# RetNet attention and a GELU feed-forward on one core: block 1's first product by seven products in all four pairs, with its sums begun earlier

## The chip, the core and the metric

The kernel runs on one core of one Trainium2 chip. The metric is the device time of one execution in microseconds (us). All data is float32.

The core has five engines with an instruction queue each. TensorE (PE in the profile) multiplies matrices, VectorE is DVE, ScalarE is ACT, GpSimd is POOL, and SyncE (SP) here only issues transfers (DMAs). POOL and ACT issue some transfers too. Each engine executes its queue in order, and an instruction that waits holds up those behind it.

## What is computed

Four batches, eight heads, 768 steps, 64 dimensions per head. First a recurrent attention, then a feed-forward with a quick GELU:

```
state = gamma[h] * state + outer(k[t], v[t])       # per batch and head, 64 x 64
y[t]  = scale * q[t] @ state
x     = y, heads side by side: 3072 tokens x 512
h     = x @ w_in                                    # 512 x 2048
g     = h * sigmoid(1.702 * h)
out   = g @ w_out                                   # 2048 x 512
```

The two weights are given in float64 and are narrowed to float32 on the chip.

## The kernel before

**Attention in steps.** The attention is computed in 24 steps; a step covers 64 time steps of two batches and all heads. `attend` (L281) holds the matmuls of a step: of step j the scores, and of step f the outputs and the state's increment. `turn` (L241) brings q and k into the transposed layout, from step 6 on with two DVE transposes (L253). `decay` (L263) scales k for the state and `aged` (L351) scales the state; both run on POOL from step 6 on (L274 and L359). `masked` (L316), `updated` (L362), `by_state` (L321) and `output` (L333) run on DVE; `output(f)` writes the step's share of x. Four steps fill a block of 512 columns of x, so there are six blocks.

**Products of a block.** A block goes through a first product (with w_in) and a second (with w_out). Weights and x are seen as 2 x 2 blocks, and instead of eight products of blocks seven are enough if sums of blocks are multiplied. From block 2 on `up(d)` (L539) does so for each of four pairs d of feature groups, and `down49` (L627) even in two levels. Block 0's first product is done plainly by `up0` (L407), its second by `down(0)` (L746).

**Block 1's first product.** It has two forms before. `up1(f)` (L420) is plain: four matmuls with 512 columns for one feature group, for f = 8 to 11, which is pair 2. Pairs 0, 1 and 3 go by `seven(d, k)` (L464): part k of pair d is four matmuls with 256 columns, recorded as eight. The parts 0, 2, 4 and 6 accumulate in one PSUM buffer "x", and after part 0, 2 and 4 ACT copies it away (L479, "kept": p1, u and vv) before the next part adds to it. Parts 1, 3 and 5 have buffers of their own, which DVE adds to the copies (L488, L494, L498, L499). `hidden` (L390) is the activation, called a gate.

`up1` and `seven` read x of block 1 from `X1`, which is W2[:, 6]. Its first half comes from steps 4 and 5, its second from steps 6 and 7. The part of the sums of x is made by `seven_x` (L433): four DVE subtractions (L439). The sums of the weights are made without DVE: `seven_w(d)` (L441) lets ACT copy three weight blocks with a sign (L450) and POOL issues DMAs that add another block to the copy (L452): w4, w6, and w5, which adds w4 and therefore waits for it to land. `seven_v(d)` (L454) copies w5 (L459) and adds a fourth block by DMA (L460): w2. Parts 2 to 5 read w5, w4, w6 and w2 in this order.

**Narrowing.** A group of weights passes through `fetch` (SP, L180, two transfers of 512 KB), `abs` (ACT, L207), `half` (three DVE operations, L211 to L213) and `rest` (three, L217 to L222). The raw weights land in three buffers in turn, so that a fetch waits for the `rest` three groups before. w0 to w7 are w_in's pairs and w8 to w15 are w_out's rows.

**The order.** Up to the end of block 1's first product the order is written out by hand: a string of names (L928 to L945), each of which calls one function. `pin` (L118) holds an instruction in this order on its engine. Operations that are not pinned are placed by a scheduler; before the change the POOL operations of `decay` and `aged` are of this kind. Behind the string, `down(0)` begins with PE at L783, and DVE makes the sums of w_out (L521 to L526) and of block 0's g (L530 to L532).

Of the kernel before, what the change touches and what calls it, by code (L numbers as in the profile page):

```python
# [12 lines left out]
ALU = mybir.AluOpType  # L13
P = 128
# [14 lines left out]
def kernel(  # L29
# [29 lines left out]
    pe, act, dve, pool, sp = nc.tensor, nc.scalar, nc.vector, nc.gpsimd, nc.sync  # L59
    ctx.enter_context(tc.manual_schedule(engines={mybir.EngineType.PE}))  # L60

    B, H, S, D = q.shape
    NT, DM = out.shape
    DFF = moe_w_in.shape[1]
    HP = H // 2
# [38 lines left out]
    cold = const.tile([P, 2 * H], F32, name="cold")  # L104
    whole = const.tile([P, HP], F32, name="whole")
    whole_h = const.tile([P, H], F32, name="whole_h")
# [5 lines left out]
    def w1(p):  # L112

        return (W1A, p) if p < NP // 2 else (W1B[p // 2 - 2], p % 2)
# [3 lines left out]
    def pin(i):  # L118
        return tc.keep_in_program_order(i) if ordered[0] else i
# [107 lines left out]
    QT, KT, KD, AT, TURNED, PA, PU, PY, SHARE = [{} for _ in range(9)]  # L227
# [3 lines left out]
    def home(j, name):  # L231

        at = ["qT", "kT", "kd", "at"].index(name)
        shape = [[HP, P] if j < NEW else [H, D]] * 2 + [[H, D], [2, HP, D]]
        shape = shape[at]
        if j >= 2 * CB:
            return one.tile([P] + shape, F32, name=name, tag=name, bufs=[2, 1, 1, 2][at])
        t = G[:, at, j % 2 * 2:j % 2 * 2 + 2].rearrange("p s t -> p (s t)")
        return t.rearrange("p (a b c) -> p a b c", a=2, b=HP) if at == 3 else t.rearrange("p (a b) -> p a b", a=shape[0])
# [23 lines left out]
    def decay(j):  # L263

        if j % NC == NC - 1:
            return
        KD[j] = home(j, "kd")
        x = QKV["kn", j]
        if j < NEW:

            for h in range(H):
                pin(act.activation(KD[j][:, h], x[:, h % HP * 2 + h // HP], AF.Copy, scale=cold[:, H + h:H + h + 1]))
        else:
            pool.tensor_mul(KD[j].rearrange("p (i s) d -> p i s d", i=2), x.rearrange("p (i s) d -> p i s d", i=2),  # L274
                            cold[:, None, H:H + HP, None].to_broadcast([P, 2, HP, D]))

    def by_half(t, j):

# [72 lines left out]
    def aged(f):  # L351

        c = f % NC
        old, new = state[c % 2], state[(c + 1) % 2]
        if f < NEW:
            for s in range(HP):
                pin(act.activation(new[:, :, s], old[:, :, s], AF.Copy, scale=whole[:, s:s + 1]))
        else:
            pool.tensor_mul(new.rearrange("p r s d -> p (r s) d"), old.rearrange("p r s d -> p (r s) d"),  # L359
                            whole_h[:, :, None].to_broadcast([P, H, D]))  # L360

    def updated(f):  # L362
        c = f % NC
# [67 lines left out]
    SUM_X, SUM_W = {}, {}  # L431
# [9 lines left out]
    def seven_w(d):  # L441

        t, q1 = w1(2 * d)
        w = [t[:, q1:q1 + 2, s].rearrange("p u c f -> p u (c f)") for s in range(4)]
        SUM_W[d] = {4: one.tile([P, 2, 2 * P], F32, name="w4", tag="qT", bufs=2),
                    5: one.tile([P, 2, 2 * P], F32, name="w5", tag="at", bufs=2),
                    6: two.tile([P, 2, 2 * P], F32, name="w6", tag="o")}
        m = SUM_W[d]
        for to, of, sign in ((4, 2, 1.0), (6, 2, -1.0), (5, 0, -1.0)):
            pin(act.activation(m[to], w[of], AF.Copy, scale=sign))  # L450
        for to, of in ((m[4], w[3]), (m[6], w[0]), (m[5], m[4])):
            pin(pool.dma_start(to, of, accum_op=ALU.add))  # L452

    def seven_v(d):  # L454

        t, q1 = w1(2 * d)
        m = SUM_W[d]
        m[2] = one.tile([P, 2, 2 * P], F32, name="w2", tag="kT")
        pin(act.activation(m[2], m[5], AF.Copy, scale=-1.0))  # L459
        pin(pool.dma_start(m[2], t[:, q1:q1 + 2, 1].rearrange("p u c f -> p u (c f)"), accum_op=ALU.add))  # L460
# [3 lines left out]
    def seven(d, k):  # L464

        t, q1 = w1(2 * d)
        a = [G[:, 2 * d:2 * d + 2, s, :] for s in range(4)]

        def product(acc, sa, sb, start, stop):
            for u in range(2):  # L470
                for c in range(2):
                    w = SUM_W[d][sa][:, u, c * P:(c + 1) * P] if sa in (4, 5, 6, 2) else t[:, q1 + u, sa, c, :]
                    x = SUM_X[sb][:, c, :] if sb in SUM_X else X1[:, sb, c, :]
                    pe.matmul(acc[:, u, :], w, x, start=(start and u == 0 and c == 0), stop=(stop and c == 1),  # L474
                              skip_group_check=True)

        def kept(name, tag, src):
            SEVEN[name] = one.tile([P, 2, TH], F32, name=name, tag=tag)
            pin(act.activation(SEVEN[name], src, AF.Copy))  # L479

        if k in (0, 1, 3, 5):
            SEVEN["x" if k == 0 else f"y{k}"] = ps.tile([P, 2, TH], F32, name="ph", tag="x" if k == 0 else "y")
        acc = SEVEN[f"y{k}" if k in (1, 3, 5) else "x"]
        product(acc, (0, 1, 5, 4, 6, 2, 3)[k], (0, 1, 5, 4, 6, 3, 2)[k], k in (0, 1, 3, 5), k in (1, 3, 5, 6))
        if k == 0:
            kept("p1", "s1", acc)
        elif k == 1:
            pin(dve.tensor_add(a[0], acc, SEVEN["p1"]))  # L488
        elif k == 2:
            kept("u", "s2", acc)  # L490
            hidden(a[0], a[0])
        elif k == 3:
            SEVEN["t"] = one.tile([P, 2, TH], F32, name="t", tag="s1")
            pin(dve.tensor_add(SEVEN["t"], acc, SEVEN["u"]))  # L494
        elif k == 4:
            kept("vv", "s3", acc)
        elif k == 5:
            pin(dve.tensor_add(a[3], SEVEN["y3"], SEVEN["vv"]))  # L498
            pin(dve.tensor_add(a[2], acc, SEVEN["t"]))  # L499
        else:  # L500
            for s in (3, 2):
                hidden(a[s], a[s])
            hidden(a[1], acc)
# [321 lines left out]
    works, products = {}, {}  # L825
# [72 lines left out]
        works[f"step-{j}"] = lambda j=j: attend(None, j)  # L898
    works["seven_x"] = seven_x
    for d in range(NP // 2):  # L900
        works |= {f"seven_w{d}": lambda d=d: seven_w(d), f"seven_v{d}": lambda d=d: seven_v(d)}
        for n in range(7):
            works[f"seven{d}.{n}"] = lambda d=d, n=n: seven(d, n)
    for i in range(2 * NFF):
        works[f"w{i // 2}{'ab'[i % 2]}"] = lambda i=i: fetch(i)
    for name, i in [("0a", 0), ("0b", 1)] + [(str(p), 2 * p) for p in range(1, NFF)]:
        n = Narrow(i)
# [20 lines left out]
    for name in """  # L928
        k0 table q0 warm turn0 w0b rows warm k1 abs0b q1 turned0 step0 v0 w0a half0b mask k2 turn1 causal rest0b
        masked0 decay0 v1 decay1 abs0a half0a step-0 updated0 turned1 q2 step1 rowd whole w2b turn2 w2a x0 k3  # L930
        aged1 masked1 turned2 v2 rest0a abs2 q3 step-1 updated1 state1 decay2 aged2 step2 q4 x1 half2 decay3 w3b
        w3a up0.0.0 masked2 turn3 k4 step-2 v3 q5 rest2 k5 gate0.0.0 turned3 updated2 state2 step3 up0.0.2
        masked3 abs3 half3 x2 rest3 turn4 w1b step-3 aged3 gate0.0.2 turned4 state3 w1a w5b updated3 v5 decay4
        abs1 x3 turn5 half1 up0.0.3 turned5 up0.1.2 step4 aged4 w5a rest1 v4 gate0.0.3 decay5 w6a masked4
        gate0.1.2 abs5 w6b step5-4 half5 rest5 up0.0.1 updated4 abs6 state4 gate0.0.1 w4b
        up0.1.1 half6 aged5 w4a up0.0.5 rest6 masked5 up0.1.5 gate0.1.1 x4 gate0.0.5 abs4 step-5 w8b w8a
        half4 gate0.1.5 state5 updated5 anew q6 up0.1.6 x5 rest4 gate0.1.6 abs8 v6 up0.0.6 w7b w7a half8
        turn6 gate0.0.6 up0.1.0 abs7 half7 gate0.1.0 w9b w9a up0.1.4 q7 gate0.1.4 decay6 step6 masked6 rest7 up0.0.4 v7
        gate0.0.4 turn7 up0.1.3 gate0.1.3 aged6 step7-6 masked7 updated6 decay7 abs9 state6 x6 up0.0.7 rest8 gate0.0.7
        w11a w11b step-7 state7 x7 seven_w0 half9 w10b w10a up0.1.7 rest9 gate0.1.7 seven_x abs11 half11  # L940
        up1.8 gate1.8 seven_v0 w12a w12b rest11 up1.9 gate1.9 abs10 seven_w1 half10 up1.10 gate1.10 w14b w14a rest10
        up1.11 abs12 gate1.11 seven0.0 seven0.1 half12 w13a w13b seven0.2 seven0.3 rest12 abs14 seven0.4 seven0.5
        half14 seven0.6 aged7 seven_v1 w15a w15b qk8 seven1.0 seven1.1 abs13 rest14 seven1.2 seven1.3 updated7 half13
        seven_w3 seven1.4 seven1.5 abs15 rest13 seven1.6 seven_v3 seven3.0 seven3.1 half15 seven3.2 seven3.3 rest15
        seven3.4 seven3.5 seven3.6 late_loads  # L945
    """.split():
        works[name]()
    ordered[0] = False
# [92 lines left out]
```

## Time and profile before

| | us |
|---|---|
| median of 3 runs | 664.78 (663.43 to 670.63) |
| the profiled execution | 664.22 |
| its span | 662.5 |
| PE busy in the span | 642.5 |
| DVE busy | 444.8 |
| POOL busy | 202.6 |
| ACT busy | 159.1 |
| PE at block 1's first product | 101.13 to 157.01 |

Positions are microseconds from the start of the span. A row of a timeline gives the start, the time to the end of the last instruction in the row, the engine, the line, what is written and read, the shape and the number of records; in brackets stands the idle time ahead of it and what ended it. A row of a stretch gives its length, then for each engine the busy time and the number of instructions, then the TensorE clock that was granted, the share of the 16 DMA engines that was busy, and GB/s.

### The profile page before, as it was taken

What the parts mean: (1) busy time and instruction counts of PE and PEld (TensorE: products, weight loads), DVE (VectorE), ACT (ScalarE), POOL (GpSimd) and SP (SyncE); (2) the same over time, 40 slices, a digit from 0 to 9 for tenths busy, and PEclk for the clock granted to TensorE, in tenths of its full rate; (3) what the DMA queues carried; (4) which work ended last, traced back from release to release, by engine and by line L of the source; (5) the groups of instructions that cost most, each with busy time, mean ns of one, the idle gap of its engine ahead of it and who ended that gap; (6) DMA issues with size and microseconds to landing.
All of it is one profiled execution on the core that took longest, in us unless ns stands there. A gap on an engine that the chain in (4) does not pass through costs nothing.

```text
span 662.5 us, 15229 instructions
## 1 busy us (share of the span) xinstructions
PE 642.5 (97%) x6366; PEld 573.6 (87%) x6366; DVE 444.8 (67%) x634; ACT 159.1 (24%) x306; POOL 202.6 (31%) x228
## 2 busy tenths in 40 slices
PE   7799999899999999999999999999999999999997
PEld 3678885788888888888999888999888999988997
DVE  3799878899735774456985445995254995254965
ACT  4774232552000000333100234010233110233110
POOL 7300321240278217100536500345600255500000
PEclk9899999899999999999999999999999999999999
DMA  9995639774403546272385832295652243602142
GB/s 184 224 258 156 190 77 265 183 147 69 76 23 141 155 120 183 52 252 96 93 221 132 268 72 96 81 219 131 200 153 96 68 148 107 228 26 96 50 158 96
DMA packets 148965, 92.65 MB, mean 140 GB/s; under 512 B 131648, under 2 KB 135232, under 8 KB 147872
## 3 DMA queue, kind: packets, MB, share of 16 engines
q1 hardware_dynamic: 135856, 45.19, 29.9%
q0 software_dynamic: 10704, 45.24, 21.2%
q10 hardware_dynamic: 2336, 1.25, 0.6%
q8 instruction: 50, 0.82, 0.5%
q14 instruction: 19, 0.16, 0.1%
HBM read 72.89 MB, written 15.47 MB: 133 GB/s over the span
## 4 chain that ended last, share of the span: by engine, by line
PE 77%; DMA 8%; issue 5%; DVE 4%; SPq 2%; POOL 2%; ACT 1%; POOLq 0%; ACTq 0%; DVEq 0%
PE pq L650 24%; PE px L546 16%; PE pd L783 13%; PE py L546 12%; PE ph L414 3%; PE ph L474 2%; PE pa L289 2%; DMA w<-w 2%; DMA G<-in_moe_w_in_dram 2%; PE py L312 1%; DMA W<-in_moe_w_out_dram 1%; PE py L306 1%; PE pa L297 1%; SPq L140 1%; DMA k_sq<-in_k_dram 1%
## 5 line engine op out<-in xcount | busy, mean ns | idle before, releaser
L619 POOL DMA_DIRECT2D ring<-W2D x28 | 15.4, 551 | 227.8 <-PE px L546 118.0
L650 PE MATMUL pq<-W,G 128*128 128x128 f32 x672 | 80.2, 276 | 0.0
L650 PEld LDWEIGHTS pq<-W,G 128*128 128x128 f32 x672 | 77.6, 192 | 0.6
L546 PE MATMUL px<-X,W1A 128*128 128x256 f32 x256 | 59.9, 379 | 0.8 <-POOL X L516 0.8
L546 PE MATMUL px<-X,W1B 128*128 128x256 f32 x256 | 59.8, 379 | 0.0
L650 PE MATMUL pq<-ring,own 128*128 128x128 f32 x448 | 59.8, 276 | 0.0
L546 PEld LDWEIGHTS px<-X,W1A 128*128 128x128 f32 x256 | 48.3, 190 | 7.6 <-POOL X L516 1.2
L650 PEld LDWEIGHTS pq<-ring,own 128*128 128x128 f32 x448 | 54.5, 192 | 0.4
L546 PEld LDWEIGHTS px<-X,W1B 128*128 128x128 f32 x256 | 48.6, 190 | 6.7
L393 ACT ACTIVATE G<-G 128x512 f32<-128x512 f32 x57 | 35.7, 630 | 59.2 <-DVE G L556 33.4
L783 PE MATMUL pd<-W,G 128*128 128x256 f32 x224 | 49.6, 381 | 0.0
L783 PEld LDWEIGHTS pd<-W,G 128*128 128x128 f32 x224 | 42.2, 190 | 5.9
L546 PE MATMUL py<-X,W1A 128*128 128x256 f32 x192 | 45.4, 379 | 0.0
L546 PE MATMUL py<-X,W1B 128*128 128x256 f32 x192 | 45.4, 379 | 0.0
L546 PEld LDWEIGHTS py<-X,W1A 128*128 128x128 f32 x192 | 36.5, 190 | 5.0
L546 PEld LDWEIGHTS py<-X,W1B 128*128 128x128 f32 x192 | 36.5, 190 | 5.0
L564 DVE TENSOR_TENSOR t<-py,u 128x512 f32<-128x512 f32 x16 | 11.1, 692 | 33.4 <-PE py L546 33.4
L553 ACT ACTIVATE p<-px 128x512 f32<-128x512 f32 x16 | 9.6, 597 | 94.5 <-PE px L546 94.5
L414 PE MATMUL ph<-X,W1A 128*128 128x256 f32 x128 | 29.0, 382 | 1.1 <-DVE X L347 0.8
L578 DVE TENSOR_TENSOR G<-G 128x512 f32<-128x512 f32 (+2 forms) x24 | 12.3, 514 | 25.7 <-ACT G L393 25.7
L650 PE MATMUL pq<-ring,G 128*128 128x128 f32 x224 | 29.6, 275 | 0.0
L650 PE MATMUL pq<-W,own 128*128 128x128 f32 x224 | 29.6, 275 | 0.0
(234 smaller groups left out, 1214.0 us busy)
## 6 DMA issues: line engine op xcount, KB each, us to landing
ring<-W2D POOLq DMA_DIRECT2D x28, 768.0 KB, 5.0
W1B<-W1D POOLq DMA_DIRECT2D x6, 1792.0 KB, 9.5
W<-in_moe_w_in_dram SPq DMA_DIRECT2D x12, 512.0 KB, 6.6
W<-in_moe_w_out_dram SPq DMA_DIRECT2D x10, 512.0 KB, 5.5
out_dram<-o POOLq DMA_DIRECT2D x20, 256.0 KB, 3.6
q_sq<-in_q_dram SPq DMA_DIRECT2D x144, 32.0 KB, 2.4
k_sq<-in_k_dram SPq DMA_DIRECT2D x144, 32.0 KB, 2.2
v_in<-in_v_dram SPq DMA_DIRECT2D x72, 64.0 KB, 3.2
```

The lines of the kernel that those rows point to most:

```text
L140: keep(engine.dma_start(*((to, at) if name == "v" else (to[:, n:H:2], at[:, n * HP:(n + 1) * HP]))))
L289: pe.matmul(pa[HALF[w], u, 0, s, :], kt[HALF[u], w, s, :], qt[HALF[u], w, s, :], start=True, stop=True)
L393: pin(act.activation(g, h[:, i], AF.Gelu_apprx_sigmoid))
L414: pe.matmul(h[:, ab], w, X[:, 2 * th + c // 2, c % 2, :], start=(ab == 0 and c == 0), stop=(c == 3), skip_group_check=True)
L474: pe.matmul(acc[:, u, :], w, x, start=(start and u == 0 and c == 0), stop=(stop and c == 1), skip_group_check=True)
L546: pe.matmul(acc[:, u, :], t[:, q1 + u, sa, c, :], X[:, sb, c, :], start=(start and u == 0 and c == 0), stop=(stop and c == 1), skip_group_ ...
L553: act.activation(p1, x, AF.Copy)
L564: dve.tensor_add(tt, z, u)
L578: dve.tensor_sub(q[0][1], q[0][0], q[0][1])
L619: pool.dma_start(c, W2D[i])
L650: pe.matmul(p0[:, j, :], a[:, d], w[:, d], start=(new and j == 0 and d == 0), stop=(d == NP // 2 - 1), skip_group_check=True)
L783: pe.matmul(p0[:, n, :], g1(m, p, sa)[:, n * P:(n + 1) * P], W2[:, sb, p, :], start=(new and p == 0 and n == 0), stop=(last and p == NP - ...
```

## The change

Pair 2 of block 1's first product goes by `seven` too, and as the first of the four, so that the order of pairs is 2, 0, 1, 3; `up1` is no longer called. `seven_w` is split: it keeps the three ACT copies, `seven_s` issues the adding DMAs of w4 and w6, and `seven_u` that of w5. For pairs 2 and 0 these stand among block 0's first product, between steps 5 and 7. `seven_x` stands right behind `output(7)` ("x7"), ahead of half9. `decay` and `aged` are pinned on POOL from step 6 on. In the string the narrowing of w9 to w15 is spread anew among the parts of `seven`.

```diff
--- before.py
+++ after.py
@@ -271,8 +271,8 @@
             for h in range(H):
                 pin(act.activation(KD[j][:, h], x[:, h % HP * 2 + h // HP], AF.Copy, scale=cold[:, H + h:H + h + 1]))
         else:
-            pool.tensor_mul(KD[j].rearrange("p (i s) d -> p i s d", i=2), x.rearrange("p (i s) d -> p i s d", i=2),
-                            cold[:, None, H:H + HP, None].to_broadcast([P, 2, HP, D]))
+            pin(pool.tensor_mul(KD[j].rearrange("p (i s) d -> p i s d", i=2), x.rearrange("p (i s) d -> p i s d", i=2),
+                                cold[:, None, H:H + HP, None].to_broadcast([P, 2, HP, D])))
 
     def by_half(t, j):
 
@@ -356,8 +356,8 @@
             for s in range(HP):
                 pin(act.activation(new[:, :, s], old[:, :, s], AF.Copy, scale=whole[:, s:s + 1]))
         else:
-            pool.tensor_mul(new.rearrange("p r s d -> p (r s) d"), old.rearrange("p r s d -> p (r s) d"),
-                            whole_h[:, :, None].to_broadcast([P, H, D]))
+            pin(pool.tensor_mul(new.rearrange("p r s d -> p (r s) d"), old.rearrange("p r s d -> p (r s) d"),
+                                whole_h[:, :, None].to_broadcast([P, H, D])))
 
     def updated(f):
         c = f % NC
@@ -448,8 +448,16 @@
         m = SUM_W[d]
         for to, of, sign in ((4, 2, 1.0), (6, 2, -1.0), (5, 0, -1.0)):
             pin(act.activation(m[to], w[of], AF.Copy, scale=sign))
-        for to, of in ((m[4], w[3]), (m[6], w[0]), (m[5], m[4])):
-            pin(pool.dma_start(to, of, accum_op=ALU.add))
+
+    def seven_s(d):
+
+        t, q1 = w1(2 * d)
+        for to, of in ((4, 3), (6, 0)):
+            pin(pool.dma_start(SUM_W[d][to], t[:, q1:q1 + 2, of].rearrange("p u c f -> p u (c f)"), accum_op=ALU.add))
+
+    def seven_u(d):
+
+        pin(pool.dma_start(SUM_W[d][5], SUM_W[d][4], accum_op=ALU.add))
 
     def seven_v(d):
 
@@ -898,7 +906,8 @@
         works[f"step-{j}"] = lambda j=j: attend(None, j)
     works["seven_x"] = seven_x
     for d in range(NP // 2):
-        works |= {f"seven_w{d}": lambda d=d: seven_w(d), f"seven_v{d}": lambda d=d: seven_v(d)}
+        works |= {f"seven_{n}{d}": lambda d=d, do=do: do(d)
+                  for n, do in (("w", seven_w), ("s", seven_s), ("u", seven_u), ("v", seven_v))}
         for n in range(7):
             works[f"seven{d}.{n}"] = lambda d=d, n=n: seven(d, n)
     for i in range(2 * NFF):
@@ -934,15 +943,15 @@
         abs1 x3 turn5 half1 up0.0.3 turned5 up0.1.2 step4 aged4 w5a rest1 v4 gate0.0.3 decay5 w6a masked4
         gate0.1.2 abs5 w6b step5-4 half5 rest5 up0.0.1 updated4 abs6 state4 gate0.0.1 w4b
         up0.1.1 half6 aged5 w4a up0.0.5 rest6 masked5 up0.1.5 gate0.1.1 x4 gate0.0.5 abs4 step-5 w8b w8a
-        half4 gate0.1.5 state5 updated5 anew q6 up0.1.6 x5 rest4 gate0.1.6 abs8 v6 up0.0.6 w7b w7a half8
-        turn6 gate0.0.6 up0.1.0 abs7 half7 gate0.1.0 w9b w9a up0.1.4 q7 gate0.1.4 decay6 step6 masked6 rest7 up0.0.4 v7
-        gate0.0.4 turn7 up0.1.3 gate0.1.3 aged6 step7-6 masked7 updated6 decay7 abs9 state6 x6 up0.0.7 rest8 gate0.0.7
-        w11a w11b step-7 state7 x7 seven_w0 half9 w10b w10a up0.1.7 rest9 gate0.1.7 seven_x abs11 half11
-        up1.8 gate1.8 seven_v0 w12a w12b rest11 up1.9 gate1.9 abs10 seven_w1 half10 up1.10 gate1.10 w14b w14a rest10
-        up1.11 abs12 gate1.11 seven0.0 seven0.1 half12 w13a w13b seven0.2 seven0.3 rest12 abs14 seven0.4 seven0.5
-        half14 seven0.6 aged7 seven_v1 w15a w15b qk8 seven1.0 seven1.1 abs13 rest14 seven1.2 seven1.3 updated7 half13
-        seven_w3 seven1.4 seven1.5 abs15 rest13 seven1.6 seven_v3 seven3.0 seven3.1 half15 seven3.2 seven3.3 rest15
-        seven3.4 seven3.5 seven3.6 late_loads
+        half4 gate0.1.5 state5 updated5 anew q6 up0.1.6 x5 rest4 gate0.1.6 seven_w2 abs8 v6 decay6 aged6 seven_s2 up0.0.6 w7b w7a half8
+        turn6 gate0.0.6 up0.1.0 abs7 half7 gate0.1.0 seven_w0 seven_u2 seven_s0 w9b w9a up0.1.4 q7 gate0.1.4 step6 masked6 rest7 up0.0.4 v7
+        gate0.0.4 turn7 up0.1.3 gate0.1.3 step7-6 masked7 updated6 decay7 aged7 seven_u0 abs9 state6 x6 up0.0.7 rest8 gate0.0.7
+        w11a w11b step-7 seven_v2 state7 x7 seven_x half9 w10b w10a up0.1.7 gate0.1.7
+        seven2.0 seven2.1 abs11 rest9 seven2.2 w12a w12b seven2.3 half11 seven2.4 abs10 seven2.5 rest11 seven2.6 seven_v0
+        w14b w14a seven0.0 seven0.1 half10 seven0.2 seven_w1 seven_s1 seven0.3 rest10 abs12 seven0.4 seven_u1 seven0.5 half12
+        w13a w13b seven0.6 seven_v1 qk8 rest12 w15a w15b seven1.0 seven_w3 seven_s3 seven1.1 abs14 seven1.2 seven1.3 half14
+        seven1.4 abs13 seven_u3 seven1.5 updated7 rest14 half13 seven1.6 seven_v3 seven3.0 seven3.1 seven3.2 abs15 seven3.3
+        rest13 seven3.4 seven3.5 half15 seven3.6 rest15 late_loads
     """.split():
         works[name]()
     ordered[0] = False
```

## The prediction

> **What bounds the kernel now.** I read the page first, then the timeline of TensorE, the waits, the timelines of POOL, SP and DVE, and stretches of the clock and the DMA share.
>
> ```profile
> span 662.5 us, 15229 instructions
> PE 642.5 (97%) x6366; PEld 573.6 (87%) x6366; DVE 444.8 (67%) x634; ACT 159.1 (24%) x306; POOL 202.6 (31%) x228
> ```
>
> TensorE (PE) is busy for 97% of the span: only fewer PE columns or fewer PE stalls can shorten it. The PE timeline of block 1's first product, with idle time ahead of a row in brackets:
>
> ```profile
> 101.13 13.90 PE L427 MATMUL ph<-W,W1B 128*128 128x512 f32 x32
> 114.87 3.62 PE L474 MATMUL ph<-W,W1A 128*128 128x256 f32 x16
> 121.11 7.13 PE L474 MATMUL ph<-x,w 128*128 128x256 f32 x24 [2.63 <-ACT p L479]
> 131.53 3.62 PE L474 MATMUL ph<-W,W1A 128*128 128x256 f32 x16
> 134.99 5.34 PE L474 MATMUL ph<-x,w 128*128 128x256 f32 x24
> 148.28 5.45 PE L474 MATMUL ph<-x,w 128*128 128x256 f32 x24 [1.04 <-ACT p L479]
> 157.01 3.62 PE L783 MATMUL pd<-W,W1A 128*128 128x256 f32 x16
> ```
>
> Pair 2 takes 114.87 - 101.13 = 13.74 us plainly. Pair 1, undisturbed, takes seven parts of 1.73 us (143.62 - 131.53 = 12.09). Pair 0 stalls for 2.6 us, and its next 24 records take 7.13 us instead of 5.34: the clock fell.
>
> ```profile
> 122.00:124.00 2.00, 2.00 (x6) 1.56 (x6) 2.00 (x3) 0.00 (x0) 0.89 (x1) 0.50 0.60 92
> ```
>
> The third number from the end is the granted clock, 0.50. The blame on the copy p (L479) is only the last link: ACT executes in order, and w2's copy (L459) stood ahead of p, waiting for an adding DMA that POOL had issued late:
>
> ```profile
> 97.55 2.54 POOL L452 DMA_DIRECT2D w<-W1A  x2 [3.50 <-ACT w L450]
> 107.56 0.88 POOL L452 DMA_DIRECT2D w<-w  x1 [7.47 <-issue]
> 143.68 0.90 POOL L452 DMA_DIRECT2D w<-w  x1 [1.26 <-DMA w<-W1B]
> ```
>
> The first two landed 10.6 and 11.8 us after issue, the third 7.3 us, the last, with a quiet queue, 3.34 us (147.03). Ahead of it all, weights w7 and w9 fill the DMA engines just where the new sums would start:
>
> ```profile
> 79.00:81.00 2.00, 2.00 (x11) 1.75 (x10) 0.28 (x1) 1.45 (x3) 0.00 (x0) 1.00 1.01 386
> 83.00:85.00 2.00, 2.00 (x31) 1.75 (x21) 1.93 (x4) 0.38 (x2) 0.00 (x0) 1.00 0.22 34
> 83.64 3.76 SPq L157 DMA_DIRECT2D k_sq<-in_k_dram  x8
> 89.44 0.71 DVE L253 STREAM_TRANSPOSE G<-k_sq 128x512 f32<-128x512 f32 x1 [1.56 <-DMA k_sq<-in_k_dram]
> 90.34 0.69 PE L289 MATMUL pa<-G 64*64 64x64 f32 x32
> ```
>
> The last but one figure of a stretch is the DMA share: 1.01, then 0.22. Step 7's k is loaded behind that, its transpose waits for it, ends at 90.15, and PE takes it at 90.34: no slack.
>
> **What the Trainium skill says.** "TensorE: Matmul & The Clock Gate", "What's actually happening": after an idle window of about 3.4 us the array runs at half clock until it has been busy for such a window, and the window runs free. The 0.50 above after a 2.6 us gap agrees; the 1.04 us gap at 147 cost no clock. "DMA: Bandwidth & Descriptors", "Issuing engines are not separate DMA queues": DMAs of SP, ACT and POOL share 16 engines. The trace agrees: in 100:105 hardware queue 69.6%, POOL's queue 35.0%. "SBUF — State Buffer", "Who interferes with whom": a DVE operation with two SBUF inputs and a POOL operation that reads SBUF shut each other out. In block 0's sums L531 takes 0.69 or 1.64 us.
>
> **The change, part by part.** All against the profiled execution (span 662.5, itself 664.2 with what lies around it; the shown median is 664.78, 0.6 above).
>
> 1. *Products.* Pair 2 goes from 16 matmuls of 512 columns (13.74) to 28 of 256 (12.10): -1.65. Its copies, additions and four gates stand on ACT and DVE beside PE work.
>
> 2. *The old stalls go.* From 101.13 to 157.01 are 55.88 us; 13.74 + 3 x 12.1 = 50.04 is work, so 5.84 is stall and slow clock. Were all four pairs gapless, they would end at 101.13 + 48.4 = 149.5: **-7.5** in all. The first two parts of pair 2 read X1's first half, ready since x5. The third needs x5 of seven_x, which moves right behind x7 (ends 99.13, sums by 101.6): ready before 104.6. The sums of pairs 2 and 0 are issued from 77 to 98 and needed after 104 and 116: even the landing of 11.8 us is hidden.
>
> 3. *Front.* seven_w2 (three ACT copies, 1.66) waits for rest4 (DVE, 73.75) and stands ahead of abs8, so abs8 moves from 72.9 to 75.4 and half8 by 2.5; DVE idled 1.88 + 0.36 there, so step 6's transposes end at about 81.5 (were 78.85), still ahead of PE's 82.6: 0. POOL runs decay6 and aged6 as now, then seven_s2 from about 77.5 to 80; u2 and s0 follow, with decay7 and aged7 pinned behind (kn lands at 91.7, s0 issued by 89: 0). But s2's bytes meet w9. One such DMA takes about 1.9 us of all engines (62.2% of 9 us for three, 116:125). With one third for POOL, the 3 us that w9 still has at 80 become 4.5: +1.5. q's last two issues wait for w9, k and kn follow on SP, and u2 and s0 share their time: k lands 1.5 to 2.5 us later, and PE stalls as long at step 7-6. v for step 7 is later too, inside the same shift. Bounds: 0 (the queues happen not to meet) to 3.5 (full serialization, 3.8). **+2.0.**
>
> 4. *Pair 1's sums.* T is pair 0's start on PE, T + 12.1 pair 1's. seven_w1 stands behind part 2's copy u, where seven_w3 stood before against pair 1, so I use its times: copies at +6.5, s1 from +7.4, w4 landed at +11.6, u1 at +12.2. Before, u landed after 3.34 (at +15.5), ACT then made w2's copy and p, and PE restarted at +16.75, 1.2 late. Now w13's 1 MB comes in the same microseconds (rest10 frees its buffer at about T + 11); the u beside w13 before (122.39) took 5.5. So PE restarts at +18.0 to +18.9 against +15.55: 2.3 to 3.3, less what the missing aged8 gives (0.5). **+2.3**; bounds 0.5 (3.34 landing) and 12 (a landing of 11.8 + 7.3). Pair 3's seven_w3 is now three parts earlier, behind 1.0: 0. Queued behind the ACT wait are p, then w3's copies and abs14, all with slack of several us.
>
> 5. *DVE.* It carries four more operations of 0.68 and is the next engine: in 99 to 157 it was 5.3 us short of full. seven_x costs it nothing new. half15/rest15 (5.85) now stand behind the last additions, so they come after E, PE's start of block 0's second product, where they came before it. DVE idled 3.15 between E and the first L530, and the next transposes (1.4) move behind it. The remainder, 0.7 plus the late L526s and a transpose, puts the last L532 at E + 28.3 to 29.3 (was 27.4). PE wants it at E + 26.6 and waited 0.8 in all: **+1.2** (0.3 to 4, by how many 0.95 us collisions with POOL fall on it). Step 8's transposes end at E + 10.0, PE wants them at 10.4: 0.
>
> 6. *SP.* w12 waits for rest9, now 3.4 us later, w14 2.7 later; both land ahead of abs12 and abs14. w15 moves behind q8 and k8 (16 issues, 8.7 us) and lands at about 140; abs15 wants it at 143: 0.
>
> Sum: -7.5 + 2.0 + 2.3 + 1.2 = -2.0; 664.2 - 2.0 = 662.2, and with half of the distance to the median **662.5**. From 160 us on the same instructions follow each other by the same triggers, so nothing more is gained or lost.
>
> **Rivals.**
>
> *Covered.* The queues hardly meet: front 0.5, pair 1 0.5, DVE 0.5. For it: POOL's share was only a third, and 85 to 95 has a share of about 0.4. Against it: the 90.15/90.34 edge. -7.5 + 1.5: **658.2**.
>
> *DVE is the bound.* It must pass rest15 and the W2 sums before block 0's sums; with three collisions in the wrong place 4 in place of 1.2: **665.3** on the same footing.
>
> *Late sums, slower.* One mechanism: pair 1's sums land as slowly as pair 0's did at 97 to 115, because w14, w13 and q8 share the engines. At 11.8 + 7.3 PE waits about 12 us at part 1.2, plus 1.8 for a half clock, where the trace showed it: -7.5 + 2.0 + 12 + 1.8 + 1.2 = +9.5, **673.7**. It turns the change into a loss once the wait passes 4.3 us. Against it: the sums at 117.84 and 122.39, beside loads too, took 4.5 and 5.5.
>
> **How the numbers follow.** Forecast 0.43, covered 0.25, DVE 0.15, late sums 0.17. The likeliest one's time stands; its own range is 660 to 665. The range of 8 in 10 takes in most of "covered" and reaches towards "late sums": 657.5 to 671. One per cent, about what a measurement of this kernel can tell from no change, is 6.6 us: below 658.1 lies half of "covered", 0.12; above 671.4 most of "late sums", 0.15; the rest is 0.73.
>
> **What would show it.** Right: no idle ahead of the third and fourth part of pair 2; a PE gap of about 2 us at step 7-6 behind k_sq's transpose; one gap of 2 to 3 us ahead of part 1.2 with ACT p as releaser and w2's copy waiting for w<-w; no gap in pair 3; PE at L791 at about 154. Wrong: step 7-6 at 90.3 as now (part 3); gapless pair 1 (part 4); a half clock in 90 to 135; or a later PE gap at the last L540, over 2 us (part 5).

## The result, and the profile after

The changed kernel takes 672.96 us (median of six runs, 670.66 to 674.19), the kernel before 664.18 (six runs, 661.38 to 670.63). The ratio is 1.0111 with a 95% interval of 1.0062 to 1.016: slower by 1.1%, 2 us above the end of the predicted range. The profiled execution took 670.79 us with a span of 669.1, so its trace explains 6.6 of the 8.8 us.

The head of the page of the changed kernel:

```profile
span 669.1 us, 15302 instructions
PE 641.6 (96%) x6390; PEld 579.1 (87%) x6390; DVE 444.8 (66%) x638; ACT 163.7 (24%) x313; POOL 209.1 (31%) x232
```

PE is busy 0.9 us less and idle 7.5 us more. Its timeline, from step 7's scores to the second product (idle time ahead in brackets; L482 is the old L474, L791 the old L783):

```profile
94.56 0.69 PE L289 MATMUL pa<-G 64*64 64x64 f32 x32 [3.79 <-DVE G L253]
97.29 4.59 PE L414 MATMUL ph<-X,W1B 128*128 128x256 f32 x16
106.93 3.62 PE L482 MATMUL ph<-W,W1B 128*128 128x256 f32 x16
119.02 3.62 PE L482 MATMUL ph<-W,W1A 128*128 128x256 f32 x16
131.10 3.62 PE L482 MATMUL ph<-W,W1A 128*128 128x256 f32 x16
140.08 7.10 PE L482 MATMUL ph<-x,w 128*128 128x256 f32 x24 [5.37 <-ACT p L487]
162.88 3.62 PE L791 MATMUL pd<-W,W1A 128*128 128x256 f32 x16
```

Pairs 2 and 0 take 12.09 and 12.08 us, without a gap. But there are two stalls, 3.79 us at step 7-6 and 5.37 us ahead of pair 1's third part, and the clock falls behind both. In these stretches the third figure from the end is the granted clock:

```profile
97.00:99.00 2.00, 2.00 (x19) 1.61 (x12) 1.62 (x4) 0.00 (x0) 2.00 (x3) 0.50 0.29 61
141.00:143.00 2.00, 2.00 (x6) 1.55 (x6) 0.00 (x0) 1.60 (x3) 2.00 (x3) 0.50 1.07 151
```

The first half clock costs about 1.66 us (the 5.45 us that the stretch from step 6 to pair 2 grew by, less the gap), the second 1.76 (pair 1's next 24 records take 7.10 us instead of 5.34). The account of the profiled execution is: up to step 6 +0.35, from there to pair 2 +5.45 (23.97 instead of 18.52), the four pairs +0.07 (55.95 instead of 55.88), from the second product on +0.73. Together that is 6.6 us.

The two stalls have one kind of cause. First the front, SP's and DVE's timelines:

```profile
85.00 6.21 SPq L157 DMA_DIRECT2D k_sq<-in_k_dram  x8
93.70 0.71 DVE L253 STREAM_TRANSPOSE G<-k_sq 128x512 f32<-128x512 f32 x1 [5.12 <-DMA kn_in<-in_k_dram]
```

Issuing k took SP 6.21 us instead of 3.76, and its transpose starts 4.3 us later. (Its row names kn_in, the load issued next, where the row of the kernel before names k_sq.) The queues between 87 and 89 us, where q0 is POOL's and q1 carries the loads (packets, MB, and the times of the packets added up as a share of 16 engines, which can pass 100%):

```profile
q0 software_dynamic: 213, 0.31, 100.6%
q1 hardware_dynamic: 280, 0.03, 11.9%
```

The kernel before had 33.3% on q1 here and nothing on q0. Then pair 1, with POOL's adding transfers, SP's load of w13 and of step 8's q, and ACT's copy behind them:

```profile
126.39 2.58 POOL L456 DMA_DIRECT2D w<-W1A  x2 [4.39 <-ACT w L450]
130.19 0.83 SPq L180 DMA_DIRECT2D W<-in_moe_w_out_dram  x2
131.07 6.57 SPq L157 DMA_DIRECT2D q_sq<-in_q_dram  x8
131.04 1.05 POOL L460 DMA_DIRECT2D w<-w  x1 [2.07 <-DMA w<-W1A]
138.92 0.63 ACT L467 ACTIVATE w<-w 128x512 f32<-128x512 f32 x1 [6.40 <-DMA w<-w]
```

The add of w4 to w5 (u1) landed 7.8 us after its issue, w2's copy waited for it, and p stood behind that copy.

### The profile page after: what moved, and what is told of

It reads as the page before. It is cut to its first block, busy times and chain, and to the rows that moved or that the text cites. A ratio compares the mean times of both kernels' runs of the same rounds, so it can differ in the third digit from the quotient of the medians.

```text
span 669.1 us, 15302 instructions
## 1 busy us (share of the span) xinstructions
PE 641.6 (96%) x6390; PEld 579.1 (87%) x6390; DVE 444.8 (66%) x638; ACT 163.7 (24%) x313; POOL 209.1 (31%) x232
## 2 busy tenths in 40 slices
DMA packets 149925, 93.70 MB, mean 140 GB/s; under 512 B 131712, under 2 KB 136064, under 8 KB 148832
## 4 chain that ended last, share of the span: by engine, by line
PE 83%; DMA 7%; issue 3%; SPq 3%; DVE 2%; POOL 0%; ACT 0%; ACTq 0%; POOLq 0%
PE pq L658 27%; PE px L554 17%; PE pd L791 15%; PE py L554 12%; PE ph L414 4%; PE ph L482 3%; PE pa L289 2%; DMA q_sq<-in_q_dram 2%; PE py L312 1%; SPq L140 1%; PE py L306 1%; DMA G<-in_moe_w_in_dram 1%; PE pa L297 1%; DMA kn_in<-in_k_dram 1%; DMA w<-w 1%
## 5 line engine op out<-in xcount | busy, mean ns | idle before, releaser
L658 PE MATMUL pq<-W,G 128*128 128x128 f32 x672 | 80.2, 276 | 0.0
L658 PEld LDWEIGHTS pq<-W,G 128*128 128x128 f32 x672 | 77.6, 192 | 0.6
L658 PE MATMUL pq<-ring,own 128*128 128x128 f32 x448 | 60.3, 277 | 1.9 <-issue 1.9
L658 PEld LDWEIGHTS pq<-ring,own 128*128 128x128 f32 x448 | 54.6, 192 | 2.7 <-issue 2.3
L393 ACT ACTIVATE G<-G 128x512 f32<-128x512 f32 x60 | 37.7, 631 | 58.9 <-DVE G L564 33.7
L791 PE MATMUL pd<-W,G 128*128 128x256 f32 x224 | 49.6, 381 | 0.0
L791 PEld LDWEIGHTS pd<-W,G 128*128 128x128 f32 x224 | 42.2, 190 | 5.8
L414 PE MATMUL ph<-X,W1B 128*128 128x256 f32 x128 | 29.9, 390 | 0.0
L658 PE MATMUL pq<-W,own 128*128 128x128 f32 x224 | 29.6, 275 | 0.0
L658 PE MATMUL pq<-ring,G 128*128 128x128 f32 x224 | 29.6, 275 | 0.0
```

Of the source, the lines that this page charges most:

```text
L393: pin(act.activation(g, h[:, i], AF.Gelu_apprx_sigmoid))
L414: pe.matmul(h[:, ab], w, X[:, 2 * th + c // 2, c % 2, :], start=(ab == 0 and c == 0), stop=(c == 3), skip_group_check=True)
L658: pe.matmul(p0[:, j, :], a[:, d], w[:, d], start=(new and j == 0 and d == 0), stop=(d == NP // 2 - 1), skip_group_check=True)
L791: pe.matmul(p0[:, n, :], g1(m, p, sa)[:, n * P:(n + 1) * P], W2[:, sb, p, :], start=(new and p == 0 and n == 0), stop=(last and p == NP - ...
```

## The experiments

The theories. **A**: the adding transfers and the loads delay each other, in two places. **B**: the front is late because seven_w2's three ACT copies push abs8, and with it half8 and the transposes. **C**: pair 1's chain of copies and adding transfers is too long for the time it has, whatever lies beside it. In experiment 4 a further rival holds that DVE takes the transfers' place as the bound. In experiment 5, **D** is that the time won is given back before the second product, and **E** that POOL's operations only collide with DVE's at another place. Edits are in the hand-written order unless said otherwise, and the lines shown of them are excerpts. Each kernel was timed beside the kernel before, whose median moved between 663.70 and 664.98 us from group to group; so differences of less than 1 us between groups are not read.

**1. Front: e1_u2s0_late and e2_all_late.** The first moves u2 and s0 behind aged7 and u0 behind v2. The second moves s2 there too, and so leaves no adding transfer ahead of step 7.

```diff
-aged6 seven_s2 up0.0.6        (e2 alone)
+aged6 up0.0.6
-gate0.1.0 seven_w0 seven_u2 seven_s0 w9b
+gate0.1.0 seven_w0 w9b
-decay7 aged7 seven_u0 abs9
+decay7 aged7 seven_u2 seven_s0 abs9    (e2: seven_s2 seven_u2 seven_s0)
-seven_v2 state7
+seven_v2 seven_u0 state7
```

> The changed kernel with u2 and s0 behind step 7's decay and aged on POOL (u0 behind w2's copy of pair 2); s2 stays at 77. Theory A (POOL's adding transfers starve step 7's q and k loads; most of it u2 and s0, which share 85 to 91 with k_sq): k_sq's issue shrinks from 6.2 us to about 4, the gap at step 7-6 from 3.8 to 1 to 2 us, the clock stays at 1.00, pair 1's gap stays at 4 to 6 us; 3 to 4 us less than the changed kernel (about 668). Theory B (the front is late because seven_w2 pushes abs8, half8 and the transposes back): the gap stays at 3.8 us and the time at 672.

> As the run before, and s2 too behind step 7's aged, so that no adding transfer runs before 94 us; the ACT copies stay where they are. Theory A: no gap at step 7-6 (under 0.5 us), clock 1.00, PE reaches pair 2 at 101.5; but w4 and w5 of pair 2 land at about 99 and 103 to 107 beside w11 and w10, so a new gap of 0 to 3 us may stand ahead of pair 2's third part; pair 1's gap stays. 667 to 670. Theory B: the gap stays at 3.8 us.

e1: 668.59 us, ratio 1.0074 (1.0045 to 1.0103), 4.4 us below the changed kernel. PE's timeline of e1, then of e2:

```profile
92.75 0.69 PE L289 MATMUL pa<-G 64*64 64x64 f32 x32 [1.21 <-DVE G L253]
136.91 7.08 PE L482 MATMUL ph<-x,w 128*128 128x256 f32 x24 [5.05 <-ACT p L487]
```

```profile
92.50 0.69 PE L289 MATMUL pa<-G 64*64 64x64 f32 x32 [0.50 <-DVE G L253]
111.50 7.86 PE L482 MATMUL ph<-x,w 128*128 128x256 f32 x24 [4.59 <-ACT p L487]
143.42 7.13 PE L482 MATMUL ph<-x,w 128*128 128x256 f32 x24 [5.07 <-ACT p L487]
```

The front's gap falls from 3.79 to 1.21 and to 0.50 us, with the copies of seven_w2 where they were: B falls, A holds for the front. In e1 no half clock follows in the front. In e2 the transfers come too late for pair 2 instead, and its time is 673.54 us, ratio 1.0141 (1.0087 to 1.0195), not the expected 667 to 670: behind aged7, s2 starts too late.

**2. Pair 1: e3_w1_early and e4_w13_late.** e3 begins pair 1's sums nearly three parts earlier (s1 at 2.5 us after pair 0's start instead of 7.4); e4 issues w13, q8 and k8 later.

```diff
-seven2.6 seven_v0                      (e3)
+seven2.6 seven_v0 seven_w1 seven_s1
-half10 seven0.2 seven_w1 seven_s1 seven0.3
+half10 seven0.2 seven_u1 seven0.3
-half12 w13a w13b seven0.6 seven_v1 qk8 rest12 w15a w15b seven1.0   (e4)
+half12 seven0.6 seven_v1 rest12 w13a w13b seven1.0
-seven1.1 abs14
+seven1.1 w15a w15b qk8 abs14
```

> The changed kernel with pair 1's ACT copies and adding transfers moved up: w1 and s1 right behind pair 2's last part, u1 behind pair 0's third part, some 8 us earlier. Theory A (u1 ran beside w13 and q8, so it landed 7.8 us after issue, and the copy of w2 held up p on ACT): pair 1's gap of 5.4 us and its half clock (1.8 us) go, the front's gap of 3.8 us stays; 665 to 667. Theory C (the chain copy, w4, w5, w2 is itself too long): a gap of over 2 us stays.

> The changed kernel with the loads of w13 moved behind rest12, and q8 and k8 behind w15's load, in pair 1; the sums stay where they are. Theory A (contention): u1 lands after 3.4 to 5 us instead of 7.8, pair 1's gap falls from 5.4 to 1 to 2.5 us and the clock stays at 1.00, so 4 to 5 us less, unless the later w13 and w15 make abs13 or rest15 late (a gap at pair 3 or at the second product up to 3 us). Theory C (chain too long by itself): the gap stays over 4 us.

Neither separated A from C, and A's times (665 to 667, and 4 to 5 us less) were missed. e3: 670.99 us, ratio 1.0103 (1.0057 to 1.015). Its s1 now ran beside w14 and took over 8 us to land; u1 therefore went out at 131.91, beside w13 as before, took 7.6 us, and the gap is 4.20 us. e4: 669.88 us, ratio 1.009 (1.0065 to 1.0116), gap 4.53 us. In e4, w13 was still issued at 129.37, because rest10 (DVE's L222, which ended at 129.35) and not SP's order releases its buffer. Its queues between 131 and 133 us:

```profile
q1 hardware_dynamic: 151, 0.57, 109.2%
q0 software_dynamic: 4, 0.00, 0.2%
```

u1, issued at 130.23, has 4 packets here at most and none from 132 to 134, while w13 moves. In the front it was POOL's queue that had the engines and the loads that waited. In both stretches the queue that was ahead had nearly everything, not a third or two thirds of it. It is not always so: from 89 to 91 us of the changed kernel q0 had 101.9% and q1 31.9%.

**3. Pair 1 with nothing beside it: e12_quiet.** rest10 stands behind pair 0's last part, so that w13 really comes later, and q8 and k8 stand behind w15.

```diff
-seven0.3 rest10 abs12 seven0.4
+seven0.3 abs12 seven0.4
-w13a w13b seven0.6 seven_v1 qk8 rest12 w15a w15b seven1.0 seven_w3 seven_s3 seven1.1 abs14
+seven0.6 seven_v1 rest10 w13a w13b rest12 w15a w15b seven1.0 seven_w3 seven_s3 seven1.1 qk8 abs14
```

> The changed kernel, with rest10 moved behind pair 0's last part, so that w13 (which needs the buffer that rest10 frees) is fetched after pair 1 has begun, and q8 and k8 behind w15. Unlike e4_w13_late, w13 and q8 are now both away while u1 is under way. A, the slow landing of u1 is made by the loads beside it: u1 lands within 3.3 to 4.5 us of its issue, the gap ahead of pair 1's part 2 falls from 5.4 to 0.8 to 1.8 us and the half clock behind it is gone: 666 to 668 us. C, the chain of copy, transfers and copy is too long by itself from where it starts: the landing stays over 6 us, the gap over 3 us with a half clock behind it, and the time over 670 us. Of either, less what a late w13 costs pair 3, up to 1 us.

PE's timeline, then two rows of the DMA issues between 133 and 139 us (KB each, median us to landing):

```profile
137.21 5.45 PE L482 MATMUL ph<-x,w 128*128 128x256 f32 x24 [0.82 <-ACT p L487]
144.75 1.97 PE L482 MATMUL ph<-W,w 128*128 128x256 f32 x8 [2.10 <-DMA w<-W1A]
153.99 5.45 PE L482 MATMUL ph<-x,w 128*128 128x256 f32 x24 [2.10 <-ACT p L487]
```

```profile
w<-W1B POOLq DMA_DIRECT2D x2, 256.0 KB, 10.6
w<-w POOLq DMA_DIRECT2D x1, 256.0 KB, 3.3
```

With quiet engines u1 lands in 3.3 us, the gap is 0.82 us and the clock holds: C falls. But w13 and w15 now meet the next adding transfers: pair 1's last sum, which PE waits 2.10 us for, and pair 3's w4 and w6, which take 10.6 us, for another 2.10. The collision moved. From step 6 to the second product the trace gains 3.5 us on the changed kernel's. Only 1.8 of them lie in the pairs; the other 1.7 are in the front, whose order is the same in both, but where no half clock followed the gap of 3.69 us this time. This execution also reached step 6 3.4 us later, and the median is 672.17 us, ratio 1.0127 (1.0068 to 1.0187): the expected 666 to 668 was missed.

**4. Sums without transfers: e5_pool1, e6_pool20, e7_pool201, e8_pool_all.** The sums of pair 1, of pairs 2 and 0, of these three, and of all four pairs are made by four POOL operations instead of ACT copies and adding transfers. No transfer of these sums is left. `seven_p` makes the first three, `seven_r` the last. In e6 to e8 seven_r0 takes the place of seven_v0, and in e8 pair 3's seven_p3 and seven_r3 take those of its copies and transfers. `seven_p` and `seven_r` move the later lines by 17: L499 is L482, L504 is L487, L808 is L791.

```diff
+    def seven_p(d):
+        ...
+        pin(pool.tensor_add(m[4], w[2], w[3]))
+        pin(pool.tensor_sub(m[5], m[4], w[0]))
+        pin(pool.tensor_sub(m[6], w[0], w[2]))
-seven0.2 seven_w1 seven_s1 seven0.3    (e5, e7, e8)
+seven0.2 seven_p1 seven0.3
-seven0.4 seven_u1 seven0.5
+seven0.4 seven0.5
-seven0.6 seven_v1 qk8
+seven0.6 seven_r1 qk8
-aged6 seven_s2 up0.0.6                 (e6, e7, e8; w2, u2, u0, v2 go)
+aged6 seven_p2 seven_r2 up0.0.6
-gate0.1.0 seven_w0 seven_u2 seven_s0 w9b
+gate0.1.0 seven_p0 w9b
```

> The changed kernel with pair 1's four sums of weights as POOL subtractions and additions, without ACT copies and without adding transfers; the other pairs as they are. Theory A (u1's transfer lands late behind w13's): pair 1's gap of 5.4 us and the half clock behind it (1.8 us) go, the front's gap (3.8 us) stays, DVE loses up to 4 us to POOL in 120 to 135 but has that much slack; 665 to 667. Theory C (the moment at which the sums start is too late whatever carries them): a gap of 2 us or more stays ahead of part 1.2.

> The changed kernel with pair 2's and pair 0's sums on POOL, at the same places in the order; no adding transfer before 115 us. Theory A: k_sq's issue and landing are as before the change, the gap at step 7-6 is under 0.5 us and pair 2 begins at about 101.5 us; pair 1's gap stays at 4 to 6 us; 667 to 668. Theory B (delay over ACT and DVE): seven_w2's ACT copies are gone too, so this run alone doesn't tell B from A, but with the run that moved u2 and s0 alone it does. POOL and DVE collide in 77 to 88: up to 3 us on DVE, behind step 6's transposes at worst 1 us of PE.

> Pairs 2, 0 and 1 on POOL, pair 3 as it is. Theory A: both gaps go; the products end at 150 to 152 us of the span, and the time is 658 to 661, below the kernel before the change. Rival (DVE takes the place of the transfers as the bound): DVE loses 6 to 8 us to collisions and PE waits for it at pairs 1 and 3 and at the second product; 663 to 666.

> All four pairs on POOL. Theory A: as with three pairs or up to 1 us less, as pair 3's sums no longer meet w15, q8 and k8; 657 to 661. Rival (DVE as the bound): 1 to 2 us more than with three pairs.

e5: 665.6 us, ratio 1.0018 (0.9996 to 1.004), 7.4 us below the changed kernel and as A expected. PE's timeline of e5:

```profile
95.89 0.69 PE L289 MATMUL pa<-G 64*64 64x64 f32 x32 [3.37 <-DVE G L253]
133.10 1.97 PE L499 MATMUL ph<-W,W1A 128*128 128x256 f32 x8 [0.35 <-DVE G L523]
135.33 5.42 PE L499 MATMUL ph<-x,w 128*128 128x256 f32 x24 [0.27 <-ACT p L504]
```

Pair 1's stall is worth what the trace said: 5.37 + 1.76 - 0.62 = 6.5 us, and the four pairs take 49.70 us instead of 55.95. The front's order is untouched; that no half clock followed its gap this time is not the edit's doing. In e6 (669.58 us, ratio 1.0092, 1.0056 to 1.0128) no adding transfer is left in the front, and still PE waits 2.55 us there, where under 0.5 was expected. DVE's timeline of e6, then of e1, shows why:

```profile
90.09 2.18 DVE L218 SCALAR_TENSOR_TENSOR W<-W,W1B 128x1024 f32<-128x1024 uint32 x1
92.31 2.17 DVE L222 TENSOR_TENSOR W1B<-W 128x1024 f32<-128x1024 f32 x1
```

```profile
85.91 1.23 DVE L218 SCALAR_TENSOR_TENSOR W<-W,W1B 128x1024 f32<-128x1024 uint32 x1
87.17 1.23 DVE L222 TENSOR_TENSOR W1B<-W 128x1024 f32<-128x1024 f32 x1
```

Beside POOL's sums DVE's two-input operations for w7 take 2.2 us instead of 1.23, so the transposes behind them are late. This agrees with the lock between DVE and POOL that "SBUF — State Buffer", "Who interferes with whom", of the Trainium skill describes. One collision was exchanged for another. e7 is e5 and e6 together: 664.13 us, ratio 1.0006 (0.9975 to 1.0037), with 2.65 us of gap left in the front. A's 658 to 661 was missed; the rival's 663 to 666 was met, but PE waits for DVE in the front, not where the rival put it. e8: 665.38 us, ratio 1.0007 (0.998 to 1.0033); with pair 3's sums on POOL as well PE waits 1.29 us for DVE (L513) in pair 1. It brings nothing, where A expected 657 to 661.

**5. The parts put together: e9_combo, e10_plain2, e11_pool_late.** e9 has e1's order for pairs 2 and 0 and e5's POOL sums for pair 1. e10 is e9 with pair 2 plain again. e11 is e7 with pair 2's POOL sums behind aged7 and pair 0's inside pair 2.

```diff
-seven2.0 seven2.1 ... seven2.6         (e10; seven_w2, s2, u2 and v2 go)
+up1.8 gate1.8 ... up1.11 gate1.11
-decay7 aged7 seven_u0 abs9             (e11)
+decay7 aged7 seven_p2 seven_r2 abs9
-abs11 rest9 seven2.2
+abs11 rest9 seven_p0 seven_r0 seven2.2
```

> Pairs 2 and 0 keep their adding transfers, in the places of e1_u2s0_late; pair 1's sums are POOL's tensor operations, as in e5_pool1. A, the adding transfers meet loads in two places and the two losses are separate: the gains add up, 4.4 us in the front and 7.4 us in pair 1, so 661.2 us at the median (ratio to the kernel before 0.995 to 0.998), with a gap of 1 to 1.5 us at step 7-6, none over 0.5 us in pair 1, and L791 at 153 to 154.5. Rival D, the time won is given back before the second product (step 8's transposes behind DVE, pair 3): 664 us or more, L791 at 156 or later.

> As e9_combo, but pair 2 has its eight plain products again and no sums of its own, so neither its ACT copies nor its four transfers are there in the front. A: TensorE has 1.65 us more to do in pair 2, and the gap at step 7-6 falls to the 0.3 to 0.6 us of the kernel before; net 0.5 to 1.2 us above e9_combo, 662 us. Rival, pair 2's sums cost more than the eighth product is worth wherever they lie: at or below e9_combo, 660.5 us.

> Pairs 2, 0 and 1 by POOL's tensor operations, as in e7_pool201, but pair 2's begin behind aged7 and pair 0's inside pair 2, so that none lies beside DVE's work for step 7. A, POOL's operations beside DVE made the 2.65 us gap of e7_pool201: the gap falls to 0.3 to 1 us and the kernel to 661.5 us. Rival E, the collision only moves: DVE's operations for w9 and w11 take 1.7 to 2.2 us instead of 1.2 us, pair 2 or pair 0 waits for its weights, and it stays at 664 us.

The scores of step 7 on PE in e9, then in e10:

```profile
93.81 0.69 PE L289 MATMUL pa<-G 64*64 64x64 f32 x32 [2.21 <-DVE G L253]
```

```profile
92.70 0.69 PE L289 MATMUL pa<-G 64*64 64x64 f32 x32 [0.31 <-DVE G L253]
```

e9: 662.78 us, ratio 0.9957 (0.9934 to 0.9981). e10: 661.69 us, ratio 0.9945 (0.9924 to 0.9965). Both beat the kernel before, whose median beside them was 664.98. The gains of e1 and e5 do nearly add up (672.96 - 4.37 - 7.36 = 661.2 expected), so A holds in both places and D does not. The gap at step 7-6 is 2.21 us, not the expected 1 to 1.5; e1 has the same order there and 1.21, so one trace tells such a gap to about 1 us only.

e10 is not behind e9, where 0.5 to 1.2 us more were expected; the rival holds. Pair 2's seven products save 1.65 us of PE work, and in these two traces the gap in the front is 2.21 - 0.31 = 1.9 us longer with them. In the best order tried, the gain of the change's main step is eaten by its own copies and transfers; the size of that is known to about 1 us.

e11: 665.45 us, ratio 1.0005 (0.9987 to 1.0023), not the 661.5 that A expected. The front has no gap, but PE waits in pair 0 for DVE, which has no pause from 97.5 us to there. PE's row, then two of DVE's:

```profile
123.32 3.24 PE L499 MATMUL ph<-W,W1A 128*128 128x256 f32 x8 [3.85 <-DVE G L523]
107.27 1.76 DVE L439 TENSOR_TENSOR x<-W 128x512 f32<-128x512 f32 x1
120.40 2.17 DVE L213 SCALAR_TENSOR_TENSOR G<-G,W 128x1024 uint32<-128x1024 uint32 x1
```

Beside POOL's sums the four subtractions L439 take 1.55 to 1.76 us each instead of 0.69 as in the changed kernel, and operations of the narrowing take about 2.2 instead of 1.23. E was right.

All traces side by side, in us; the last two columns are the time from step 6's scores on PE to the second product, and the part of it from the start of the four pairs on. Four pairs without any gap would take 48.4, or 50.0 with pair 2 plain.

| kernel | median | gap at step 7-6 | gaps in the pairs | step 6 to second product | the four pairs |
|---|---|---|---|---|---|
| before | 664.18 | none | 2.63, 1.04 | 74.4 | 55.9 |
| changed | 672.96 | 3.79 | 5.37 | 79.9 | 56.0 |
| e1_u2s0_late | 668.59 | 1.21 | 0.26, 5.05, 0.82 | 76.7 | 56.9 |
| e2_all_late | 673.54 | 0.50 | 4.59, 5.07 | 82.0 | 62.9 |
| e3_w1_early | 670.99 | 4.30 | 4.20 | 78.8 | 54.5 |
| e4_w13_late | 669.88 | 3.46 | 4.53 | 78.2 | 56.2 |
| e12_quiet | 672.17 | 3.69 | 0.82, 2.10, 2.10 | 76.4 | 54.1 |
| e5_pool1 | 665.6 | 3.37 | 0.35, 0.27 | 71.7 | 49.7 |
| e6_pool20 | 669.58 | 2.55 | 4.95 | 77.5 | 56.3 |
| e7_pool201 | 664.13 | 2.65 | 0.27 | 70.6 | 49.3 |
| e8_pool_all | 665.38 | 2.65 | 0.27, 1.29 | 74.0 | 51.2 |
| e9_combo | 662.78 | 2.21 | 0.44, 0.27 | 70.7 | 49.9 |
| e10_plain2 | 661.69 | 0.31 | 0.39, 0.27 | 70.3 | 51.4 |
| e11_pool_late | 665.45 | none | 0.71, 3.85 | 73.8 | 55.1 |

## Why the prediction was wrong

1. *Products, old stalls.* Right. Pair 2 takes 12.09 us, and pairs 2 and 0 run without a gap as forecast.
2. *Front (+2.0).* The place and the waiting transpose were right, the size was not: +5.45. The failed step is "u2 and s0 share their time: k lands 1.5 to 2.5 us later". k's transpose started 4.3 us later (93.70 instead of 89.44), and PE stood for 3.79. What s2 does by way of w9 and q, forecast at 1.5 with one third for POOL, came out about right: with u2 and s0 away, a gap of 1.21 (e1) or 2.21 us (e9) is left. The rest, 1.6 to 2.6 us, is k waiting behind u2 and s0, for which the range left at most 1.0 (2.5 less 1.5). From 87 to 89 us q0 had 100.6% and q1 11.9%: nearly the case that the text called full serialization, priced at 3.8. On top came 1.66 us of half clock, which the sum did not hold, although the "late sums" rival priced 1.8 for one. A half clock in 90 to 135 was named as a sign of being wrong, and it came. Whether it comes is partly chance: e12, e4 and e5 have the same order up to there, gaps of 3.69, 3.46 and 3.37 us, and no half clock behind them.
3. *Pair 1 (+2.3).* The chain and its start were right: s1 at T + 7.4 (forecast + 7.4), u1 at T + 12.0 (+ 12.2), with T at 119.02. The failed term is the landing of u1, taken as at most 5.5 us from one transfer of the kernel before; it took 7.8, with w13 and q8 issued in the same microsecond. e12 shows that alone it is 3.3. Gap and half clock come to 7.1 us, 4.8 more than forecast: 2.1 by the later landing, 1.8 by the half clock, and about 1 because the sum took the low end of its own range. This is the "late sums" rival's mechanism at about half its price. That its 673.7 lies so near the 672.96 measured is luck: the front cost 3.4 us more than the rival took for it, and the median lies 2.2 us above the profile. The wait is past the rival's turning point of 4.3 us, which leaves out the half clock that the rival itself counts; with it the turning point is 2.5.
4. *DVE (+1.2).* Too high: no gap is left at the last L540, where the kernel before had 0.8 us in all. (From 99 to 157 us DVE was busy for 51.58 of 58 us there, so 6.4 us short of full and not 5.3.) From the second product on the profile is 0.73 us longer; the two largest gaps there are 0.89 and 1.05 us in the two-level products (L658), which the trace gives to "issue", and the kernel before has one of 0.79 us, for POOL (L516). No run here tells their cause.
5. *Start and median.* Up to step 6 PE has the same instructions in the same order, yet step 6 began at 82.61 us in the kernel before and between 82.96 and 86.32 in the other thirteen profiles. The difference arises before 22 us, some 50 us before the first edited piece of the order runs: the first step's scores begin within 1 us of each other in all fourteen, the second step's at 18.81 us in the kernel before and between 19.10 and 21.56 in the others. And the changed kernel's median lies 2.2 us above its profiled execution, where the kernel before had none. Why this is so stays open.

The sum with the measured terms: -2.0 + 3.45 (front) + 5.27 (the four pairs, -5.2 forecast and +0.07 found) - 0.47 (behind them) + 0.35 (start) = +6.6. The two errors are of one kind: what an adding transfer and the loads beside it do to each other was carried over from another moment, as an average share or as one landing time, and the chains that wait for it have no slack. In both places the half clock that a wait can bring was left out of the sum.

## What to carry to other kernels

Before work is moved onto a DMA queue, look at what the queues do in exactly those microseconds, and count the load on the path as waiting for the whole transfer, not for a share of it; and count a possible half clock, here 1.6 to 3.2 us, to any TensorE gap of 2.6 us or more. When the sums of a faster product cost transfers on a path without slack, price them first: here the saved 1.65 us were gone even in the best order tried. Replacing transfers by an engine's operations paid where the other engine had slack, in pair 1, and not in the front.

## What the runs showed of the hardware

- An adding transfer of 256 KB within SBUF lands 3.3 us after its issue on quiet engines, 7.8 beside a weight load, 10.6 beside two. "DMA: Bandwidth & Descriptors", "Anatomy of one DMA — SWDGE (gpsimd) path", of the Trainium skill gives 2.0 us plus bytes over 436 GB/s, an estimate of 2.6 us for it; the 3.3 measured count here.
- POOL's queue and the loads do not share evenly: 100.6% to 11.9% in one stretch, 0.2% to 109.2% in another, 101.9% to 31.9% in a third.
- Whether the clock falls is not told by the gap alone. Between step 7-6 and the second product it fell after all ten gaps of 3.79 us and more, after two of the seven from 2.55 to 3.69 (2.63 in the kernel before, 2.65 in e8, but not after the same 2.65 in e7), and after none of 2.21 or less. Where 24 records stand behind such a gap in the pairs, they took 6.92 to 8.49 us instead of 5.34. The free-running window of "TensorE: Matmul & The Clock Gate", "What's actually happening", in the Trainium skill fits the mixed middle, but not the falls after 2.63 and 2.65 us, which are shorter than its idle window of about 3.4; so the prediction was wrong to call the 2.6 us an agreement.
- A POOL sum of 128x512 took 1.26 us at best (e7) and up to 2.29 beside DVE (e8).
